# Gated attention mix: the order and form of the first loads, of the first maxima, and of the filler blocks

## The chip, the core and the metric

The kernel runs on one core of a Trainium2 chip. Its time is device time in microseconds (us), the median of several runs. One execution of each kernel is also profiled; the rows shown below come from that execution. TensorE (PE) multiplies matrices into eight PSUM banks of 128x512 fp32, VectorE (DVE) and ScalarE (ACT) read them out, GpSimd (POOL) works between SBUF tiles, and DMA transfers are issued from the queues of SyncE (SP), ACT and POOL.

## The reference

```python
x = A_x                                     # 1 x 2048 x 576, fp32
g = sigmoid((x * gate_w).sum(-1))           # one gate for each row
a = softmax(qa @ ka.T * 18**-0.5) @ va      # 32 heads of 18, each with its own q, k, v
b = softmax(qb @ kb.T * 18**-0.5) @ vb      # 32 heads of 18, with one shared k and v
return g * (a @ A_wo) + (1 - g) * (b @ B_wo)
```

All of it is in fp32. There are 64 heads in all over 2048 keys and 2048 queries; the 32 heads with shared keys come first.

## The kernel before, in words

**Precision and tiling.** A number is split into a high part (the fp32r rounding) and a low part (what the rounding left), and a product is made of three partial products. x comes transposed (576 x 2048). The weights are cut into 14 tiles of 128 output columns ("mt"): tile 0 holds the shared k, the gate, the shared v and the first q rows, tiles 1 to 4 the other q rows of the shared heads, tiles 5 to 13 the q and k rows of the other heads. The contraction over 576 is four chunks of 128 rows and a tail of 64 rows. The tail is loaded twice, into partitions 0 to 63 and 64 to 127 of a fifth chunk, and the upper copy is turned into the low part (`last_x`, `last_w`), so that one matmul does both. `load5` (L244) loads a tile: the four chunks in one transfer ("main"), the tail in two of 64 rows ("rest").

**The first stage** (to about 37 us) projects weight tile 0 for all four column chunks of 512, and tile 1 for the first two. It needs the weight tiles W0 and W1 (`wst`), two x tiles of 256 columns (`xsh`, here x0 and x1) and three of 512 columns (`xs`, here xs2, xs3 and xs4). A tile is split on ACT (high), on DVE (low) and on POOL or DVE (tail). `project` (L265) does one weight tile on one chunk of x, 28 matmuls of 256 columns where `parts` is 2; `leave_first` and `leave` (L295, L290) split the result and write it to memory (`kq`, `kd`, `ke`, `qk`); `first_back` and `rows_back` (L343, L351) read the rows back as the operands of scores (`qs`, `ksb`, `kdb`, `keb`). Both run on SP's queue, which is strictly in order. A DMA that is issued on SP also waits until the transfer eight before it, counted over SP's and ACT's queues together, has landed.

**The lead** (37 to about 75 us) finds row maxima of head 0 and of part of head 1 before the first scores. It is a string of letters (L1142) that `lead_steps` plays. A pair "x", "y" finds the maximum over two key chunks at once: x multiplies with the difference of the two chunks and ACT takes its relu, y multiplies with one chunk and DVE adds the relu and takes the maximum. "A" and "B" are single matmuls of the remaining projections (tile 1's other half, tile 2), on the two halves of the array. `pairs` (L1080) gives the order of the 47 pairs as (first row tile, which two chunks); row tiles 0 to 15 are head 0. After pair (15, 1), `max_rows(0)` turns head 0's maxima into a row that the score matmuls read: DVE, a split on POOL, then two DMAs in a chain, `m_d<-mh` and `qs<-m_d` (L711, L714). "v" makes the shared v.

**The main loop** runs 1024 steps T (16 key tiles of 64 heads). Eight steps are a block: a string of 32 score matmuls "s" (each read out by an exp on ACT), 48 maxima "m" or pairs "x"/"y" for a head 22 steps on (read out by DVE), and the sums over v (the digits). Blocks differ in how many *units* of other work their string holds as A and B: PLAIN none, HALF14 and HALF12 one, TWO14 and TWO12 two, DENSE four. A unit is one 128x292 piece of the other rows' projection (`row_units`), of the values (`value_units`) or of the output projection (`out_proj`). The loop at L1229 picks the string by T. Units for weight tiles 5 to 13 ("the other rows") begin at `RB` = 266, their first loads and splits 8 steps earlier, and `TWICE` gives five of their blocks two units; the output projection begins after `RE` = 730.

Of the kernel before, what the change touches and what calls it, by code (L numbers as in the profile page):

```python
# [8 lines left out]
F32 = mybir.dt.float32  # L9
# [8 lines left out]
S = 2048  # L18
# [138 lines left out]
def gated_mix_kernel(ctx: ExitStack, tc: tile.TileContext, xT, wall, wv, wo, out):  # L157
# [85 lines left out]

    def load5(t, src, rest=None, main=None):  # L244
        dma(t[:, 0:4, :], src[0:512, :].rearrange("(p k) m -> p k m", p=P), main)
        dma(t[0:64, 4, :], src[512:576, :], rest)
        dma(t[64:128, 4, :], src[512:576, :], rest)

    def split_w(st, w, eng_l):
        nc.scalar.activation(w["h"], st, AF.Copy)  # L250
# [88 lines left out]
    def back(t, i, b, x0, x1):  # L339
        n = 64 if i < 3 else 54  # L340
        dma(t[b:b + n, x0:x1], kq_d[54 * i:54 * i + n, x0:x1])

    def first_back():  # L343
        back(ksb, 0, SB, 0, 512)
        back(qs[0], 1, SB, 0, 1024)
        back(qs[0], 1, MB, 0, 1024)
        load_kd(kdb, ROW_KB)
        for b in (MB, SB):
            back(qs[1], 2, b, 0, 1024)

    def rows_back():  # L351
        back(ksb, 0, SB, 1024, 1536)
        dma(keb[MB:MB + 54, :], ke_d.rearrange("p a f -> (p a) f"))
        for b in (MB, SB):
            back(qs[0], 1, b, 1024, S)
        for f in REST_ROWS:
            f()
        for b in (MB, SB):
            back(qs[1], 2, b, 1024, S)
        for b in (SB, MB):  # L360
            for x in (512, 1536):
                back(ksb, 0, b, x, x + 512)
            dma(ksb[b + 54:b + 56, :], ones_r)
        for x in (0, 1024):
            back(ksb, 0, MB, x, x + 512)
        dma(z, z_d.rearrange("(p f) -> p f", p=P))
        for b in (MB, SB):
            back(qs[2], 3, b, 0, S)

    REST_ROWS = []  # L370

    with tc.tile_pool(name="xs", bufs=1, side="right") as xsp:
        XS = []

        def load_x(c, rest=None, main=None):
            half = c < 2
            XS.append(xsp.tile([P, NKT, 256 if half else 512], F32, name="xsh" if half else "xs", bufs=2 if half else 3))
            if main:
                nc.vector.memset(XS[c][0:1, 0:1, 0:1], 0.0)
                nc.vector.memset(XS[c][0:1, 4:5, 0:1], 0.0)  # L380
# [12 lines left out]

        def split_x(c):
            xs = XS[c // 2 + 1][:, :, 256 * (c % 2):256 * (c % 2) + 256] if c > 1 else XS[c]
            cs = slice(c * 256, (c + 1) * 256)
            nc.scalar.activation(X["h"][:, :, cs], xs, AF.Copy)
            low_x(c, xs)
            last_x(c, xs)

        def low_x(c, xs):
            cs = slice(c * 256, (c + 1) * 256)
            nc.vector.tensor_tensor(X["l"][:, :, cs], xs[:, 0:4], X["h"][:, 0:4, cs].bitcast(F32), op=OP.subtract)

        def last_x(c, xs):
            xh = X["h"][64:128, 4, c * 256:(c + 1) * 256]
            (nc.gpsimd if c > 1 else nc.vector).tensor_tensor(xh, xs[64:128, 4], xh.bitcast(F32), op=OP.subtract)

        W = [load_w(0, nc.scalar)]
        load_x(0, nc.scalar)  # L410
        nc.scalar.activation(ones, ones, AF.Copy)
        load_x(1, nc.gpsimd)
        W.append(load_w(1, nc.gpsimd))

        warm = in_turn("m")
        for i in range(6):
            nc.tensor.matmul(warm[:, 0:304], ident, vb.rearrange("p k d -> p (k d)"), start=True, stop=True)
        for c in range(2, 4):
            load_x(c)
        dma(ones_r.rearrange("a (b c) -> (a b) c", c=32), ones)  # L420

        x0, xh = XS[0], X["h"][:, :, 0:256]
        ST = [W.pop(0) for _ in range(2)]
        WP = [main_w(ST[0])]
        nc.scalar.activation(xh[:, 0:2], x0[:, 0:2], AF.Copy)
        nc.vector.tensor_copy(xh[:, 2:4], x0[:, 2:4])
        low_x(0, x0)
        last_w(ST[0], WP[0])
        nc.scalar.activation(xh[:, 4], x0[:, 4], AF.Copy)
        last_x(0, x0)  # L430
        split_x(1)
        WP.append(prep_w(ST[1]))
        load_x(4, nc.gpsimd, nc.gpsimd)
        W.append(load_w(2))

        def chunk(c):
            split_x(2 * c)
            split_x(2 * c + 1)

        F = project(0, 0, WP[0], 2)  # L440
        REST_ROWS.append(leave_first(0, F))
        F = project(1, 0, WP[1], 2)
        chunk(1)
        leave(1, 0, F)
        F = project(0, 1, WP[0], 2)
        REST_ROWS.append(leave_first(1, F))
        first_back()
        F = project(1, 1, WP[1])
        chunk(2)
        leave(1, 1, F)  # L450
        F = project(0, 2, WP[0], 2)
        split_x(6)
        REST_ROWS.append(leave_first(2, F))
        split_x(7)
        F = project(0, 3, WP[0], 2)
        REST_ROWS.append(leave_first(3, F))
        rows_back()
        WP.append(prep_w(W.pop(0)))

# [596 lines left out]
        when(16 * (last_head(t) + 1) + 5, lambda t=t: slow.append(normalise(t)))  # L1056
    when(16 * (NU - 1) + 4, lambda: run(normalise(8, at_end=True)))
    VA = 10 + 8 * (7 * (RA - NT) + 1)
    RB = VA + 8 * 17
    RE = 730  # L1060
    TWICE = [VA + 8 * n for n in range(16)] + [RB + 88 * n for n in range(5)]
    when(2, lambda: begin_units(row_units(NT, RA)))
    when(VA - 8, lambda: (early("vx"), begin_units(value_units())))
    when(RB - 8, lambda: (early("px"), begin_units(row_units(RA, MT))))
    when(RE, open_oacc)
    SEG = ((0, [P] * 4, RE - 8, RE), (4, [P] * 4, 930, 942))
    for t0, rows, Ta, Tb in SEG:
# [5 lines left out]
    def keep_busy():  # L1073

        for n in (512, 256):
# [1 line left out]
                             start=True, stop=True, skip_group_check=True)  # L1077

    pos = {"s": 0, "P": 0, "x": (LEAD + 2) // 2, "y": (LEAD + 2) // 2}
    pairs = {"x": [(M, h) for M0, h in ((0, 0), (16, 0), (0, 1), (8, 0), (8, 1), (16, 1))  # L1080
                   for M in range(M0, M0 + 8)][:-1]}
    pairs["y"] = list(pairs["x"])

# [16 lines left out]
    def lead_max(what, low):  # L1100
        M, h = pairs[what].pop(0)
        u, i = divmod(M, 16)
        b = SB if low else MB
        pm = bank_tile(clk.bank(what, 0 if low else 1))
        k = (kdb, keb)[h][b:b + 54, :] if what == "x" else ksb[b:b + 54, 1024 * h:1024 * h + 512]
        nc.tensor.matmul(pm, qs[u][b:b + 54, i * P:(i + 1) * P], k, start=True, stop=True)  # L1106
        if what == "x":
            MX["x", M, h] = lead.tile([P, 512], F32, name="xb", bufs=2) if (M, h) == (LEAD, 1) else \
                xdp.tile([P, 512], F32, name="xd", bufs=4)
            nc.scalar.activation(MX["x", M, h], pm, AF.Relu)  # L1110
            return
        if u not in MX:
            MX[u] = mxs[u]
        junk = lead.tile([P, 512], BF16, name="junk", bufs=1) if (M, h) == (LEAD, 1) else \
            xdp.tile([P, 512], BF16, name="junk2", bufs=3)
        nc.vector.tensor_tensor_reduce(junk, pm, MX.pop(("x", M, h)), 1.0, -3e38, op0=OP.add, op1=OP.max,  # L1116
                                       accum_out=MX[u][:, i, 2 * h:2 * h + 1])
        if (M, h) == (15, 1):
            max_rows(0)

    def lead_steps(ops):

        for op in ops.replace(" ", ""):
# [12 lines left out]
            else:  # L1136
# [2 lines left out]
    last_m = [(LEAD + 1, 2), (LEAD + 1, 3)]  # L1139
    clk.half = STREAM  # L1140
    begin_units(lead_units())
    lead_steps("xABABxyABxyABABxyABABxyABxyABABxyABABxyABxyABABxyABABxyABxyA"  # L1142
               "BABxyABABxyABxyABABxyABABxyABxyABABxyABABxyABxyABABxyABABxyA"
               "BxyABABxyABABxyABxyABABxyABxyvABABxyABABxyABxyABABxyABABxyAB"
               "xyABABxyABABxyABxyABABxyABABxyABxyABABxyABABxyABABxyABABxyAB"
               "ABxyABxyABByBBBBBssssssmsms")
    clk.half = HALF_MM

    PLAIN = "mssmsm 4 smsmsm 3 smmssx 3 smmsys 3 mssxysm 3 msxmssm 3 mssysms 3 msssmys 4 msmsms 3 smxssm 3"
# [79 lines left out]
    while pos["s"] < 4 * (NSTEP - LEAD):  # L1229
# [3 lines left out]
        if T >= SEG[1][3] + 4:  # L1233
            emit(DENSE, 4)
        elif T in TWICE:
            emit(TWO14, 2)
        elif 10 <= T < RE and T + 8 not in (VA, RB):
            emit(HALF14, 1)
        elif RE + 8 <= T < RE + 8 * 9:
            emit(TWO12, 2)  # L1240
        elif RE + 8 * 9 <= T < RE + 8 * 25:
            emit(HALF12, 1)
        else:
            emit(PLAIN)
# [42 lines left out]
```

## Time and profile before

| what | us |
|---|---|
| median of 3 runs (lowest, highest) | 2651.08 (2648.82, 2652.03) |
| the profiled execution: its time | 2647.61 |
| the profiled execution: its span, first to last instruction | 2645.8 |
| PE busy | 2625.2 (99% of the span) |
| ACT busy | 2448.1 (93%) |
| DVE busy | 2392.7 (90%) |
| POOL busy | 948.4 (36%) |

The granted TensorE clock over the whole span is 0.997 of full speed. A row of the timeline reads: start, duration, engine, line, operation, what is written from what, count, and in brackets the idle time of the engine before it with what ended it. A row of the windows reads: the stretch, its length, busy time and count of each engine, the granted clock, the mean busy share of the 16 DMA engines, and GB/s.

### The profile page before, as it was taken

How to read it: one execution, taken by the hardware profiler on the slowest of the kernel's cores; microseconds unless marked ns; L12 is line 12 of the kernel's file. 1: busy time of each engine (PE TensorE's matmuls, PEld its weight loads, DVE VectorE, ACT ScalarE, POOL GpSimd, SP SyncE). 2: the span in 40 equal slices, each digit the busy share in tenths (PEclk: the TensorE clock that was granted, in tenths of full speed). 3: DMA queues.
4: the chain of work that ended last, by engine and by line, in shares of the span. 5: the costliest groups of instructions: out<-in, count | busy, mean ns of one | idle time of the engine just before them, and what ended most of it. 6: DMA issues, size and time to landing. Idle time of an engine off the chain costs nothing.

```text
span 2645.8 us, 67415 instructions
## 1 busy us (share of the span) xinstructions
PE 2625.2 (99%) x25371; PEld 1412.3 (53%) x25371; DVE 2392.7 (90%) x4571; ACT 2448.1 (93%) x4864; POOL 948.4 (36%) x1195
## 2 busy tenths in 40 slices
PE   8999999999999999999999999999999999999999
PEld 6545555555545455455555555554555554545665
DVE  6899999999989999999999999999989999999883
ACT  6999999999989999999999999999999999999887
POOL 4444331211056454735475447544310020012113
PEclk9999999999999999999999999999999999999999
DMA  7422222221144234333544445434422332223322
GB/s 224 124 84 79 83 78 74 88 63 56 55 126 129 89 103 118 111 104 104 145 141 147 123 120 174 143 103 128 147 86 83 93 98 88 64 84 121 115 57 92
DMA packets 186091, 280.81 MB, mean 106 GB/s; under 512 B 59929, under 2 KB 147305, under 8 KB 174513
## 3 DMA queue, kind: packets, MB, share of 16 engines
q1 hardware_dynamic: 169301, 221.95, 29.2%
q0 software_dynamic: 15424, 53.03, 5.4%
q8 instruction: 200, 3.28, 0.5%
q10 hardware_dynamic: 1040, 1.52, 0.2%
q14 instruction: 126, 1.03, 0.1%
HBM read 200.74 MB, written 66.90 MB: 101 GB/s over the span
## 4 chain that ended last, share of the span: by engine, by line
PE 96%; DMA 1%; POOL 1%; issue 0%; SPq 0%; DVE 0%; ACT 0%; ACTq 0%; POOLq 0%; DVEq 0%
PE acc L749 38%; PE bank L689 28%; PE bank L734 18%; PE bank L957 11%; PE acc L761 1%; PE bank L937 1%; PE bank L1106 0%; DMA m_d<-mh 0%; SPq L163 0%; DMA xst<-xT 0%; DMA qs<-m_d 0%; POOL oacc L930 0%; POOL wrl L242 0%; DVE junk L1116 0%; POOL xr L552 0%
## 5 line engine op out<-in xcount | busy, mean ns | idle before, releaser
L742 ACT ACTIVATE pt<-bank 128x512 f32<-128x512 f32 x4096 | 2153.9, 616 | 143.3 <-PE bank L734 77.1
L698 DVE TENSOR_REDUCE mx<-bank 128x1 f32<-128x512 f32 x3002 | 1890.2, 684 | 138.9 <-PE bank L734 68.9
L734 PE MATMUL bank<-qs,ksb 56*128 56x512 f32 x2688 | 916.2, 425 | 4.3 <-DMA qs<-m_d 4.3
L689 PE MATMUL bank<-ksb,qs 54*128 54x512 f32 x2270 | 821.5, 427 | 0.0
L749 PE MATMUL acc<-pt,vb 128*19 128x128 f32 (+3 forms) x6064 | 552.0, 460 | 0.0
L689 PEld LDWEIGHTS bank<-ksb,qs 54*128 54x128 f32 x2270 | 386.5, 185 | 286.2 <-ACT pt L742 148.1
L749 PE MATMUL acc<-pt,vg 128*19 128x256 f32 (+3 forms) x5936 | 534.6, 456 | 0.0
L734 PEld LDWEIGHTS bank<-qs,ksb 56*128 56x128 f32 x2688 | 443.9, 185 | 167.1 <-DVE mx L698 65.6
L734 PE MATMUL bank<-qs,ksa 56*128 56x512 f32 x1408 | 467.9, 425 | 0.0
L689 PE MATMUL bank<-ksa,qs 54*128 54x512 f32 x1232 | 438.7, 426 | 0.0
L695 DVE CUSTOM_DVE_ANT_0 junk<-bank,xb 128x512 bf16<-128x512 f32 x500 | 342.8, 686 | 30.1 <-PE bank L734 25.5
L692 ACT ACTIVATE xb<-bank 128x512 f32<-128x512 f32 x500 | 294.7, 606 | 12.5 <-PE bank L734 3.8
L689 PEld LDWEIGHTS bank<-ksa,qs 54*128 54x128 f32 x1232 | 207.8, 184 | 151.1 <-ACT pt L742 86.9
L734 PEld LDWEIGHTS bank<-qs,ksa 56*128 56x128 f32 x1408 | 225.8, 184 | 84.7 <-DVE mx L698 31.7
L240 POOL CAST rhl<-rst 128x292 fp32r<-128x292 f32 (+2 forms) x95 | 40.0, 421 | 552.7 <-issue 378.6
L749 PEld LDWEIGHTS acc<-pt,vb 128*19 128x19 f32 x6064 | 122.3, 97 | 215.7 <-issue 186.9
L240 POOL CAST mh<-mt 128x32 fp32r<-128x32 f32 x63 | 13.2, 210 | 614.6 <-DVE mt L707 506.6
L749 PEld LDWEIGHTS acc<-pt,vg 128*19 128x19 f32 x5936 | 119.5, 97 | 208.9 <-issue 183.6
L957 PE MATMUL bank<-xr,wrh 64*128 64x292 f32 (+1 forms) x1386 | 202.9, 300 | 0.0
L957 PEld LDWEIGHTS bank<-xr,wrh 64*128 64x128 f32 x1386 | 169.7, 187 | 3.1
L689 PE MATMUL bank<-kdb,qs 54*128 54x512 f32 x372 | 160.5, 431 | 0.0
L552 POOL TENSOR_TENSOR xr<-xst,xr 128x876 fp32r<-128x876 f32 (+1 forms) x77 | 159.4, 2070 | 0.0
(171 smaller groups left out, 2432.5 us busy)
## 6 DMA issues: line engine op xcount, KB each, us to landing
qs<-qk SPq DMA_DIRECT2D x366, 144.0 KB
xst<-xT SPq DMA_DIRECT2D x66, 438.0 KB
qk<-rhl POOLq DMA_DIRECT2D x66, 292.0 KB, 4.2
ksa<-qk SPq DMA_DIRECT2D x132, 144.0 KB
xst<-xT SPq DMA_DIRECT2D x66, 146.0 KB
xst<-xT SPq DMA_DIRECT2D x132, 73.0 KB
ksb<-qk SPq DMA_DIRECT2D x60, 144.0 KB
onh<-oh POOLq DMA_DIRECT2D x32, 256.0 KB, 3.3
```

The source lines that it names most:

```text
L240: eng_h.tensor_copy(h, src)
L552: nc.gpsimd.tensor_tensor(x[:, 5:8, 0:n], t0, x[:, 0:3, 0:n].bitcast(F32), op=OP.subtract)
L689: nc.tensor.matmul(pm, qs[u % 3][b:b + 54, i * P:(i + 1) * P], k, start=True, stop=True)
L692: nc.scalar.activation(MX["x", u, i], pm, AF.Relu)
L695: nc.vector.tensor_tensor_reduce(junk, pm, MX.pop(("x", u, i)), 1.0, -3e38, op0=OP.add, op1=OP.max, accum_out=MX[u][:, i, c:c + 1])
L698: nc.vector.tensor_reduce(MX[u][:, i, c:c + 1], pm, axis=AX.X, op=OP.max)
L734: nc.tensor.matmul(ps, kst(u)[b:b + 56, i * P:(i + 1) * P], qs[u % 3][b:b + 56, c * 512:(c + 1) * 512], start=True, stop=True)
L742: nc.scalar.activation(pt, ps, AF.Exp, scale=SCALE)
L749: nc.tensor.matmul(acc[32 * j:32 * j + 19, a:b], v_of(u, i), PT[u, i, j][:, a:b], start=(i == 0), stop=(i == 15), skip_group_check=True)
L761: nc.tensor.matmul(acc[32 * j:32 * j + 19, 256 * half + a:256 * half + b], v_of(NU - 1, i), pt[:, x + a:x + b], start=(i == 0), stop=(i == ...
L937: nc.tensor.matmul(fp[:, 0:u.n], x, y, start=(n == 0), stop=(n == len(u.ops) - 1))
L957: nc.tensor.matmul(u.fp[op][:, 0:u.n], x[b:b + 64], y[b:b + 64], start=(n == 0), stop=(n == last))
```

## The change

The line numbers in the program move by up to 7.

- `load5` loads a tail with one transfer of 128 rows, whose source is the 64 rows with a leading dimension of two copies, in place of two transfers of 64 rows. All its callers get this: the first loads, the weight tiles of the other rows (`wrst`), and x for the values.
- W1 and x1 are loaded in the order W0, x0, W1, x1, with all four tails on ACT's queue; W1's and x1's tails were on POOL's. The loads of xs4 and of W2 and the write of `ones_r` are issued later.
- The first projections go tile 0 and tile 1 on x0, then both on x1; two idle matmuls follow. xs4 is split in one piece.
- The reads back go in another order, head 0's first, and `second_back` reads 512 columns earlier.
- In the lead, head 0's 32 pairs come first, `max_rows(0)` splits on DVE, and the A and B stand elsewhere between the pairs.
- `RB` goes from 266 to 274 while the units' first loads stay at T = 258; the block at T = 266 becomes PLAIN; the five extra two-unit blocks become one-unit blocks; `RE` goes from 730 to 778, and 14 blocks of TWO12 and 4 of HALF12 follow in place of 8 and 16.

```diff
     def load5(t, src, rest=None, main=None):
         dma(t[:, 0:4, :], src[0:512, :].rearrange("(p k) m -> p k m", p=P), main)
-        dma(t[0:64, 4, :], src[512:576, :], rest)
-        dma(t[64:128, 4, :], src[512:576, :], rest)
+        m = src.shape[1]
+        dma(t[:, 4, :], src[512:576, :].unsqueeze(0).to_broadcast([2, 64, m]), rest)
...
+    def back2(t, i, x0, x1):
+        for b in (SB, MB):
+            back(t, i, b, x0, x1)
+
     def first_back():
+        back2(qs[0], 1, 0, 1024)
         back(ksb, 0, SB, 0, 512)
-        back(qs[0], 1, SB, 0, 1024)
-        back(qs[0], 1, MB, 0, 1024)
         load_kd(kdb, ROW_KB)
-        for b in (MB, SB):
-            back(qs[1], 2, b, 0, 1024)
+
+    def second_back():
+        back2(qs[0], 1, 1024, 1536)
 
     def rows_back():
+        dma(keb[MB:MB + 54, :], ke_d.rearrange("p a f -> (p a) f"))
+        back2(qs[0], 1, 1536, S)
         back(ksb, 0, SB, 1024, 1536)
...
         W = [load_w(0, nc.scalar)]
         load_x(0, nc.scalar)
+        W.append(load_w(1, nc.scalar))
+        load_x(1, nc.scalar)
         nc.scalar.activation(ones, ones, AF.Copy)
-        load_x(1, nc.gpsimd)
-        W.append(load_w(1, nc.gpsimd))
...
+        WP.append(prep_w(ST[1]))
         split_x(1)
-        WP.append(prep_w(ST[1]))
-        load_x(4, nc.gpsimd, nc.gpsimd)
-        W.append(load_w(2))
...
-        F = project(0, 0, WP[0], 2)
-        REST_ROWS.append(leave_first(0, F))
-        F = project(1, 0, WP[1], 2)
+        F = [in_turn("g") for _ in range(2)]
+        for x in (0, 256):
+            for mt in range(2):
+                products(F[mt], WP[mt], 0, x, 256)
+        idle(2)
+        REST_ROWS.append(leave_first(0, F[0]))
         chunk(1)
-        leave(1, 0, F)
+        load_x(4, nc.gpsimd, nc.gpsimd)
+        leave(1, 0, F[1])
         F = project(0, 1, WP[0], 2)
         REST_ROWS.append(leave_first(1, F))
         first_back()
+        W.append(load_w(2))
+        dma(ones_r.rearrange("a (b c) -> (a b) c", c=32), ones)
         F = project(1, 1, WP[1])
         chunk(2)
         leave(1, 1, F)
         F = project(0, 2, WP[0], 2)
-        split_x(6)
+        chunk(3)
         REST_ROWS.append(leave_first(2, F))
-        split_x(7)
+        second_back()
         F = project(0, 3, WP[0], 2)
...
     VA = 10 + 8 * (7 * (RA - NT) + 1)
-    RB = VA + 8 * 17
-    RE = 730
-    TWICE = [VA + 8 * n for n in range(16)] + [RB + 88 * n for n in range(5)]
+    RB = VA + 8 * 18
+    RE = 778
+    TWICE = [VA + 8 * n for n in range(16)]
...
-    when(RB - 8, lambda: (early("px"), begin_units(row_units(RA, MT))))
+    when(RB - 16, lambda: (early("px"), begin_units(row_units(RA, MT))))
...
-    pairs = {"x": [(M, h) for M0, h in ((0, 0), (16, 0), (0, 1), (8, 0), (8, 1), (16, 1))
+    pairs = {"x": [(M, h) for M0, h in ((0, 0), (8, 0), (0, 1), (8, 1), (16, 0), (16, 1))
                    for M in range(M0, M0 + 8)][:-1]}
...
         if (M, h) == (15, 1):
-            max_rows(0)
+            max_rows(0, nc.vector)
...
-        elif 10 <= T < RE and T + 8 not in (VA, RB):
+        elif 10 <= T < RE and T + 8 not in (VA, RB, RB - 8):
             emit(HALF14, 1)
-        elif RE + 8 <= T < RE + 8 * 9:
+        elif RE + 8 <= T < RE + 8 * 15:
             emit(TWO12, 2)
-        elif RE + 8 * 9 <= T < RE + 8 * 25:
+        elif RE + 8 * 15 <= T < 930:
             emit(HALF12, 1)
```

What moves, at three places. First ACT's queue at the start of the program: wst_118 is W0, xsh_122 (now xsh_121) is x0, xsh_127 is x1, wst_131 (now wst_124) is W1. Before:

```order
L163 DMA wst_118<-wall 64x128 x2
L163 DMA xsh_122<-xT 64x256 x2
L411 ACT_TABLE_LOAD
L411 ACTIVATE ones_96<-ones_96 128x32
L386 ACTIVATE wh_151<-wst_118 128x512
L425 ACTIVATE xh_113<-xsh_122 128x2x256
L391 ACTIVATE wh_151<-wst_118 128x128
L429 ACTIVATE xh_113<-xsh_122 128x256
L397 ACTIVATE xh_113<-xsh_127 128x5x256
L250 ACTIVATE wh_165<-wst_131 128x640
```

With the change:

```order
L163 DMA wst_118<-wall 128x1x128
L163 DMA xsh_121<-xT 128x1x256
L163 DMA wst_124<-wall 128x1x128
L163 DMA xsh_127<-xT 128x1x256
L413 ACT_TABLE_LOAD
L413 ACTIVATE ones_96<-ones_96 128x32
L386 ACTIVATE wh_144<-wst_118 128x512
L428 ACTIVATE xh_113<-xsh_121 128x2x256
L391 ACTIVATE wh_144<-wst_118 128x128
L432 ACTIVATE xh_113<-xsh_121 128x256
L250 ACTIVATE wh_155<-wst_124 128x640
L397 ACTIVATE xh_113<-xsh_127 128x5x256
```

There are still four transfers on ACT's queue, but now one for each tail: x0's is the second, x1's the fourth. ACT splits W1 before x1.

Second, PE's first projections: bank0 is tile 0's result, bank1 tile 1's; wh_151 and wl_152 (now wh_144 and wl_145) are W0, the other pair is W1. Before, from x1's part of tile 0 on:

```order
L277 MATMUL bank0_179<-xh_113,wh_151 128x256 x4
L277 MATMUL bank0_179<-xh_113,wl_152 128x256 x4
L277 MATMUL bank0_179<-xl_114,wh_151 128x256 x4
L277 MATMUL bank0_179<-xh_113,wh_151 128x256
L277 MATMUL bank0_179<-xh_113,wl_152 128x256
L277 MATMUL bank1_218<-xh_113,wh_165 128x256 x4
L277 MATMUL bank1_218<-xh_113,wl_166 128x256 x4
```

With the change, from the same place:

```order
L277 MATMUL bank1_163<-xh_113,wh_155 128x256 x4
L277 MATMUL bank1_163<-xh_113,wl_156 128x256 x4
L277 MATMUL bank1_163<-xl_114,wh_155 128x256 x4
L277 MATMUL bank1_163<-xh_113,wh_155 128x256
L277 MATMUL bank1_163<-xh_113,wl_156 128x256
L277 MATMUL bank0_162<-xh_113,wh_144 128x256 x4
L277 MATMUL bank0_162<-xh_113,wl_145 128x256 x4
```

Tile 1's part on x0 now stands ahead of both parts on x1.

Third, SP's queue where the units of the other rows begin (T = 258 and 266): `wrst` is a weight tile, `xst` a piece of x, `R` and `r_d` belong to a normalisation, `m_d_73` and `qs_92` carry the maxima of head 17, whose scores begin at T = 272. Before:

```order
L163 DMA wrst<-wall 128x512
L163 DMA wrst<-wall 64x128 x2
L163 DMA r_d<-sm 112x128
L163 DMA R<-r_d 16x2048
L163 DMA R<-r_d 18x2048 x6
L163 DMA R<-r_d 4x2048
L163 DMA m_d_73<-mh 128x64
L163 DMA qs_92<-m_d_73 1x64x32 x2
L163 DMA xst<-xT 128x3x292
L163 DMA xst<-xT 128x292
```

With the change:

```order
L163 DMA wrst<-wall 128x512
L163 DMA wrst<-wall 128x1x128
L163 DMA r_d<-sm 112x128
L163 DMA R<-r_d 16x2048
L163 DMA R<-r_d 18x2048 x6
L163 DMA R<-r_d 4x2048
L163 DMA m_d_73<-mh 128x64
L163 DMA qs_92<-m_d_73 1x64x32 x2
L163 DMA qs_91<-qk 18x2048 x6
L163 DMA ot<-oe 18x512 x4
```

Everything up to the maxima of head 17 stands in the order it had, with one transfer fewer; the third piece of x comes after it.

More of the change, by code (lines that the diff above doesn't have):

```diff
@@ L341, in back @@
         dma(t[b:b + n, x0:x1], kq_d[54 * i:54 * i + n, x0:x1])
+    def back2(t, i, x0, x1):
+        for b in (SB, MB):
+            back(t, i, b, x0, x1)
     def first_back():
+        back2(qs[0], 1, 0, 1024)
         back(ksb, 0, SB, 0, 512)
-        back(qs[0], 1, SB, 0, 1024)
-        back(qs[0], 1, MB, 0, 1024)
         load_kd(kdb, ROW_KB)
-        for b in (MB, SB):
-            back(qs[1], 2, b, 0, 1024)
+    def second_back():
+        back2(qs[0], 1, 1024, 1536)
     def rows_back():
+        dma(keb[MB:MB + 54, :], ke_d.rearrange("p a f -> (p a) f"))
+        back2(qs[0], 1, 1536, S)
         back(ksb, 0, SB, 1024, 1536)
-        dma(keb[MB:MB + 54, :], ke_d.rearrange("p a f -> (p a) f"))
-        for b in (MB, SB):
-            back(qs[0], 1, b, 1024, S)
         for f in REST_ROWS:
             f()
-        for b in (MB, SB):
-            back(qs[1], 2, b, 1024, S)
+        back2(qs[1], 2, 0, S)
+        for x in (512, 1536):
+            back(ksb, 0, SB, x, x + 512)
+        back(ksb, 0, MB, 0, S)
         for b in (SB, MB):
-            for x in (512, 1536):
-                back(ksb, 0, b, x, x + 512)
             dma(ksb[b + 54:b + 56, :], ones_r)
-        for x in (0, 1024):
-            back(ksb, 0, MB, x, x + 512)
         dma(z, z_d.rearrange("(p f) -> p f", p=P))
-        for b in (MB, SB):
-            back(qs[2], 3, b, 0, S)
+        back2(qs[2], 3, 0, S)
     REST_ROWS = []
@@ L406, in last_x, with idle @@
             xh = X["h"][64:128, 4, c * 256:(c + 1) * 256]
-            (nc.gpsimd if c > 1 else nc.vector).tensor_tensor(xh, xs[64:128, 4], xh.bitcast(F32), op=OP.subtract)
+            (nc.gpsimd if c > 1 and c % 2 == 0 else nc.vector).tensor_tensor(xh, xs[64:128, 4], xh.bitcast(F32), op=OP.subtract)
         W = [load_w(0, nc.scalar)]
         load_x(0, nc.scalar)
+        W.append(load_w(1, nc.scalar))
+        load_x(1, nc.scalar)
         nc.scalar.activation(ones, ones, AF.Copy)
-        load_x(1, nc.gpsimd)
-        W.append(load_w(1, nc.gpsimd))
         warm = in_turn("m")
-        for i in range(6):
-            nc.tensor.matmul(warm[:, 0:304], ident, vb.rearrange("p k d -> p (k d)"), start=True, stop=True)
+        def idle(n):
+            for i in range(n):
+                nc.tensor.matmul(warm[:, 0:304], ident, vb.rearrange("p k d -> p (k d)"), start=True, stop=True)
+        idle(6)
         for c in range(2, 4):
             load_x(c)
-        dma(ones_r.rearrange("a (b c) -> (a b) c", c=32), ones)
         x0, xh = XS[0], X["h"][:, :, 0:256]
@@ L1141, in gated_mix_kernel @@
     begin_units(lead_units())
[L1142 to L1146, printed above, removed]
+    lead_steps("xABABxyABxyABABxyABxyABABxyABABxyABxyABABxyABABxyABxyABABxyA"
+               "BxyABABxyABABxyvABxyABABxyABABxyABxyABABxyABxyABABxyABABxyAB"
+               "xyABABxyABxyABABxyABABxyABxyABABxyABABxyABxyABABxyABABxyABAB"
+               "xyABABxyABABxyABABxyABABxyABABxyABABxyABABABxyABABxyABABxyAB"
+               "ABxyABBxyBBxyBByBssssssmsms")
     clk.half = HALF_MM
```

## The prediction

> **What bounds the kernel now.** I read the page's chain of waits first, then score matmuls by block, the clock in short windows, and last the timelines of the start.
>
> ```profile
> PE 96%; DMA 1%; POOL 1%; issue 0%; SPq 0%; DVE 0%; ACT 0%; ACTq 0%; POOLq 0%; DVEq 0%
> 354.10:373.51 19.41, 10.65 (x32) 5.21 (x32) 1.00 0.08 24
> 373.51:392.06 18.55, 10.68 (x32) 5.22 (x32) 1.00 0.56 160
> 475.63:496.44 20.81, 11.24 (x32) 5.37 (x32) 1.00 0.20 65
> 1904.55:1925.32 20.77, 11.11 (x32) 5.30 (x32) 1.00 0.45 127
> 2089.32:2108.91 19.59, 10.87 (x33) 5.27 (x33) 1.00 0.22 66
> 744.10:769.82 25.72, 11.91 (x33) 5.65 (x33) 0.93 0.52 141
> 1610.80:1632.35 21.55, 11.32 (x33) 5.37 (x33) 1.00 0.36 99
> 79.63:100.68 21.05, 12.39 (x33) 5.88 (x33) 0.88 0.44 129
> ```
>
> The chain is PE nearly throughout. The other rows are windows of the score line (L734), each one block of 32 score matmuls: HALF14 takes 19.41, PLAIN 18.55, TWO14 20.81, TWO12 20.77, HALF12 19.59 (a late one; its neighbours take 19.4). So a first unit in a block costs about 0.87 and a second about 1.4. Three blocks are off: T = 266 (a TWO14, 25.72), T = 618 (a TWO14, 21.55), and T = 2 (a PLAIN, 21.05). The change touches these and the first stage; between them PE is full and only the mix of blocks counts.
>
> **Part 1: the first loads.** Where the first stage waits now:
>
> ```profile
> 6.52 0.63 ACT L425 ACTIVATE xh<-xsh 128x512 fp32r<-128x512 f32 x1 [0.96 <-DMA xsh<-xT]
> 11.71 0.42 ACT L429 ACTIVATE xh<-xsh 128x256 fp32r<-128x256 f32 x1 [4.36 <-DMA xsh<-xT]
> 12.03 1.25 ACT L397 ACTIVATE xh<-xsh 128x1280 fp32r<-128x1280 f32 x1
> 12.63 0.39 PE L277 MATMUL bank<-xh,wh 128*128 128x256 f32 x1 [3.43 <-DVE xh L407]
> 34.96 0.74 PE L277 MATMUL bank<-xh,wh 128*128 128x256 f32 x4 [1.45 <-ACT xh L397]
> 37.50 0.49 PE L1106 MATMUL bank<-kdb,qs 54*128 54x512 f32 x1 [0.20 <-DMA kdb<-kd]
> ```
>
> x0's main part is there at 6.52, its tail, the last two of ACT's four small transfers, at 11.71, and x1 right behind it; PE loses 3.4 us. The first pair of the lead starts at 37.50. The change wants the tails sooner. What they cost in their new form depends on how many of the 16 DMA engines one transfer uses. The trace has transfers with different outer dimensions almost alone:
>
> ```profile
> 734.00:738.00 4.00, 4.00 (x42) 2.14 (x38) 3.92 (x8) 4.00 (x9) 0.92 (x1) 1.00 0.98 305
> 751.00:757.00 6.00, 6.00 (x62) 3.74 (x60) 5.96 (x11) 5.00 (x10) 1.81 (x4) 1.00 0.57 143
> 61.60:62.50 0.90, 0.90 (x12) 0.77 (x10) 0.90 (x3) 0.79 (x2) 0.71 (x1) 1.00 0.07 18
> q1 hardware_dynamic: 4, 0.02, 7.0%
> ```
>
> With x tiles of 128 rows in flight the engines are 0.98 busy; with `R<-r_d`, whose source is one row broadcast to 18, the share is 0.57, which is 9 of 16, the largest divisor of 18 that 16 engines hold; the third stretch is one `ksb<-ones_r` of 2 rows of 8 KB, the last row its queue: four packets, 7% of 16 engines for 0.90, or 1.0 engine-us, two engines for half a us. So the outer dimension sets the count, a leading broadcast dimension included. The new tail has a source of 2 x 64 rows whose first dimension is a broadcast of 2, and a destination of 128 rows. No row has a transfer whose two sides differ so; I take the smaller side, **two engines**, and keep 16 as a rival. (The Trainium skill, DMA: Bandwidth & Descriptors, in the section "Why a DMA increments its semaphore by 16 and not by 1", says that the number of engines is the largest up to 16 that divides the slowest dimension of both sides, and elsewhere names a leading zero-stride broadcast as what confines a copy. The counts of 9 and 2 above agree with it, and by it the tails run on two engines. It speaks against this change.)
>
> Price: the 2-row transfer moves 8 KB per engine in 0.49 us, 16.6 GB/s; the 128-row window gives 305/(0.98 x 16) = 19.5 GB/s. Two engines carry 31 to 39 GB/s. ACT's four tails are 64 + 128 + 64 + 128 = 384 KB, so 10 to 13 us from the start of transfers near 2, if nothing else uses those engines: x1's tail at 12 at the earliest. But SP's queue uses the same engines: an eighth of its 3584 KB of mains (448 KB) and both 256 KB tails of xs2 and xs3. All 1344 KB would take until 37 to 46. SP holds some of that back, since an issue waits for the landing of the transfer eight before it:
>
> ```profile
> 3.73 8.38 SPq L163 DMA_DIRECT2D xs<-xT  x6
> L163 SPq DMA_DIRECT2D xs<-xT x6: 465/516/1612, 3.7 to 11.6; - x6
> L163 POOL DMA_DIRECT2D xs<-xT x3: 529/534/797, 16.2 to 17.5; - x3
> DMA to landing us min/median/max: 9.0/9.2/9.3
> ```
>
> six issues of about half a us stretch over 8.38, and now xs2 waits for W0's tail and xs3 for x0's. With one packet of SP's between two of ACT's, counted packet by packet, I get W0's tail at 9, x0's at 15, W1's at 22, x1's at 30. I take **30**, with 20 and 39 as ends. PE cannot put it off: both tiles need x1 before anything else can follow. ACT's split of x1 then goes from 12.03 to 30: **+18** (+8 to +27).
>
> From there to the first pair takes 25.5 now. Tile 1's 14 matmuls on x0 are done by then, and x7's split no longer stands behind a readout, which saves most of the 1.45 at 34.96. Against it, xs4's load moves from 16.17, 4.1 after x1's split, to behind the splits of xs2, some 10.3 after it. It took 9.0 to 9.3 to land (last rows above), so ACT, ready for it about 16 after x1, waits till 19.5. Net **+1.5** (0 to +3). Order of reading back: head 0's columns 1024 to 2047 are wanted by pairs 8 and 12, now 16 pairs sooner; their cover is the ten pairs ahead, at 0.7 us each, and if the last read came late it would cost about 1, inside the ends.
>
> **Part 2: the lead's end.**
>
> ```profile
> 71.00 0.35 SPq L163 DMA_DIRECT2D m_d<-mh  x1
> 73.40 1.25 SPq L163 DMA_DIRECT2D qs<-m_d  x2
> 74.28 0.69 DVE L1116 CUSTOM_DVE_ANT_0 junk<-bank,xb 128x512 bf16<-128x512 f32 x1
> 76.41 0.93 PE L734 MATMUL bank<-qs,ksb 56*128 56x512 f32 x3 [1.18 <-DMA qs<-m_d]
> 75.50:77.00 1.50, 0.59 (x4) 0.53 (x5) 0.00 (x0) 0.52 (x2) 0.98 (x1) 1.00 0.81 293
> 78.00:80.00 2.00, 2.00 (x7) 1.44 (x6) 1.38 (x2) 2.00 (x5) 1.66 (x2) 0.50 0.06 25
> 82.00:84.00 2.00, 2.00 (x10) 0.50 (x4) 1.05 (x2) 1.08 (x3) 0.00 (x0) 0.50 0.16 53
> ```
>
> The first score waits 1.18 for the maxima of head 0. About 2 us later the granted clock halves and stays so to about 84; the block at T = 2 takes 21.05, 2.5 over a PLAIN. With head 0's pairs first, `max_rows(0)` stands 15 pairs before the end, 10 us, against the 5.4 from `m_d<-mh` at 71.00 to 76.41, so the DMAs are covered. The split on DVE adds two ops of about 0.2, inside the ends. The sum of A, B, x and y is unchanged. I take **-3.7**: the wait and the slow clock behind it. (The Trainium skill, TensorE: Matmul & The Clock Gate, Part 1, puts the drop behind an idle window of about 3.4 us. The idle stretch here is 1.18 and the clock still falls. By the rule alone only the 1.2 would come back, and the sum below would be +19.3.)
>
> **Part 3: the blocks.** From T = 266 to 922, five TWO14 and twelve HALF12 become ten HALF14, six TWO12 and one PLAIN: 5 x 20.81 + 12 x 19.4 = 336.9 against 10 x 19.41 + 6 x 20.77 + 18.55 = 337.3, or +0.4; the TWO14 at T = 618 was 0.7 over its kind, which goes: -0.3. At T = 266:
>
> ```profile
> 745.20 2.92 SPq L163 DMA_DIRECT2D wrst<-wall  x3
> 752.57 0.34 SPq L163 DMA_DIRECT2D m_d<-mh  x1
> 759.78 1.25 SPq L163 DMA_DIRECT2D qs<-m_d  x2
> 762.60 0.47 PE L734 MATMUL bank<-qs,ksb 56*128 56x512 f32 x1 [3.09 <-DMA qs<-m_d]
> ```
>
> head 17's maxima are issued at 752.57, land 7.2 later behind 1 MB of `R<-r_d`, and PE waits 3.09 at 762.60. SP's order up to there is the same, so the free block does not bring them sooner: it brings PE's need sooner, to 744.1 + 0.75 x 18.55 = 758.0, a wait of 4.6 with 1.5 of slow clock, 24.7 in all for 25.72, of which 20.81 was work. The block's two units are priced above, so its loss over its kind goes from 4.9 to 6.1: +1.2. One issue less on SP gives up to 1 back; W's tail of 64 KB on two engines in front of R costs 1.7 to 2.1. Together **+1** (-4, were the wait gone, to +3).
>
> **The sum.** +18 + 1.5 - 3.7 + 1 = +16.8 on the profiled execution's own time of 2647.6 (span 2645.8 and 1.8 around it): 2664.4. The median of the runs shown stands 3.5 higher, at 2651.08, so I predict **2668** for the median. The tail's break-even is 13 us: landing then, x1 would be 1.2 late, and the sum is zero.
>
> **The rivals.**
> *Faster: the tails run on all 16 engines*, as the destination's 128 rows would have it. Now ACT's fourth transfer is seen at 11.71, 2.7 each from 0.75; as the second, x0's would be there near 7 and PE's 3.4 us wait at 12.63 would go. x1's would still come near 10.9; with xs4 later than now the first pair comes 3.2 sooner. With -3.7 and -1 (no late tail at T = 266): -8, **2643**. For it: the form saves transfers, and the destination is an ordinary one. Against it: the share of 0.57 on a leading broadcast.
> *No change: two engines, but ACT's queue served first.* Then x1's tail lands near 14: +2 + 1.5 - 3.7 + 1 = +0.8, **2652**. For it: 10 to 13 us of bytes are all it needs. Against it: the engines are 0.98 busy when SP's mains run, and the tail's packets must stand in line.
> The free block that removes the wait at 762.60 is worth 4 more on any of these; nothing in SP's order speaks for it.
>
> **How the numbers follow.** Two engines with SP's packets between: 0.68, own range 2657 to 2677 (x1's tail from 20 to 39); 16 engines: 0.22; two engines, short: 0.10. A measurement can tell about 0.2% (5.3 us) from no change. The first case lies above that nearly always (0.66, and 0.02 within), the second below it in 0.19 (0.03 within), the third within in 0.06 and 0.02 on either side. Slower 0.68, same 0.11, faster 0.21. The range of 2643 to 2677 holds some 0.6 of the first case, the third and half of the second, 0.8 in all.
>
> **What would show it.** Right: on ACT, the split of x0's tail begins after 13 and that of x1 (five chunks, 128x1280) near 30, both ended by a DMA; DMA share well under 0.5 between 15 and 30; the first pair near 57; no idle PE before the first score and a T = 2 block near 18.6; T = 266 still waiting for `qs<-m_d`. Wrong: x0's tail split before 9, or x1's before 13; then the outer dimension of the source does not confine a transfer, and the loss of part 1 is a gain.

## The result, and the profile after

The changed kernel takes 2676.12 us (median of four, 2671.24 to 2677.71) against 2649.95 (2646.59 to 2652.03): 1.0097 times as long, with a 95% interval of 1.0079 to 1.0114. It is slower by about 26 us. The forecast was slower, 2668 in a range of 2643 to 2677. Its sum was +16.8 on the profiled execution; that of the changed kernel has a span of 2673.9 (2675.66 with what lies around it), 28.1 more than the 2645.8 before. So the direction and the main cause came out, and 11 us are missing.

The page's chain of waits of the changed kernel, whose share of DMA was 1% before:

```profile
PE 94%; DMA 3%; POOL 1%; DVE 1%; SPq 0%; issue 0%; ACT 0%; ACTq 0%; POOLq 0%
```

The timeline of its first loads and first stage (start, duration, engine, line, and in brackets the idle time before and who ended it), and one window of it (length, busy time of each engine, then clock, DMA share, GB/s). The line of a five-tile split is L397 as before, the first splits of x0 are three lines further down, pairs are L1113, scores L741:

```profile
3.29 6.58 ACTq L163 DMA_DIRECT2D xsh<-xT  x1
13.70 0.42 ACT L432 ACTIVATE xh<-xsh 128x256 fp32r<-128x256 f32 x1 [1.04 <-DMA xsh<-xT]
21.31 0.74 ACT L250 ACTIVATE wh<-wst 128x640 fp32r<-128x640 f32 x1 [7.19 <-DMA wst<-wall]
29.51 1.27 ACT L397 ACTIVATE xh<-xsh 128x1280 fp32r<-128x1280 f32 x1 [7.47 <-DMA xsh<-xT]
25.00:30.00 5.00, 0.46 (x3) 0.17 (x1) 0.00 (x0) 0.49 (x1) 0.00 (x0) 0.84 0.13 47
41.15 1.65 POOL L163 DMA_DIRECT2D xs<-xT  x2 [1.95 <-DVE xs L380]
53.83 2.43 ACT L397 ACTIVATE xh<-xs 128x1280 fp32r<-128x1280 f32 x2 [7.02 <-DMA xs<-xT]
60.66 0.50 PE L1113 MATMUL bank<-kdb,qs 54*128 54x512 f32 x1
```

x0's tail, then W1's, then x1's land one after the other, each ending an idle ACT. From 25 to 30 the DMA share is 0.13, two of 16 engines, at 47 GB/s. x1's tail does not have these two to itself. The queues from 20 to 25 (packets, MB, share of 16 engines):

```profile
q1 hardware_dynamic: 81, 0.16, 9.0%
q10 hardware_dynamic: 82, 0.08, 4.4%
```

q10 is ACT's queue (its 0.39 MB by 29.5 are the four tails), q1 is SP's, where only the tails of xs2 and xs3 have this form. They take turns, packet by packet. ACT itself stands on its fourth issue until 9.87 (first row of the timeline), so its first split, of W0, starts at 11.33 instead of 4.95; what holds the issue the trace does not say, and the late x1 hides it. Then ACT waits again, for xs4, and the first pair starts at 60.66 instead of 37.50.

The lead in the timelines of PE and SP, with one window for the clock:

```profile
69.66 0.26 SPq L163 DMA_DIRECT2D keb<-ke  x1
70.03 1.75 SPq L163 DMA_DIRECT2D qs<-kq  x2
74.28 0.76 PE L1113 MATMUL bank<-kdb,qs 54*128 54x512 f32 x1 [2.75 <-DMA qs<-kq]
76.00:78.00 2.00, 2.00 (x12) 1.22 (x11) 0.93 (x3) 0.96 (x2) 0.00 (x0) 0.50 0.98 298
104.69 0.40 PE L741 MATMUL bank<-qs,ksb 56*128 56x512 f32 x1
```

The first score waits for nothing any more. But in the middle of the lead the thirteenth pair waits 2.75 for the last 512 columns of head 0's queries, and the clock is at half from 74 to 82. The lead, first pair to first score, takes 44.03 where it took 38.91.

Not all of this is the change. One of the kernels below, the probe, differs from the changed kernel only behind its last output. In its execution x1's split and the first pair come at 29.53 and 60.32, nearly as here, but the same pair waits 1.88, the clock stays at 1.00 behind it (it is at half only earlier, from about 66 to 69), and the lead takes 40.75 (its thirteenth pair and its first score):

```profile
74.31 0.47 PE L1113 MATMUL bank<-kdb,qs 54*128 54x512 f32 x1 [1.88 <-DMA qs<-kq]
101.07 1.32 PE L741 MATMUL bank<-qs,ksb 56*128 56x512 f32 x5
```

Blocks, as windows of the score line (the last row is the kernel before, its last block):

```profile
107.85:128.29 20.44, 11.59 (x32) 5.36 (x32) 1.00 0.42 118
771.75:796.82 25.07, 11.77 (x32) 5.61 (x33) 0.86 0.37 104
2584.59:2607.66 23.07, 11.74 (x33) 5.56 (x34) 1.00 0.17 54
2556.36:2579.43 23.07, 11.72 (x32) 5.56 (x32) 1.00 0.17 54
```

T = 2 takes 20.44 with the clock at full speed; T = 266, now a PLAIN, still takes 25.07; T = 618 is an ordinary HALF14 (19.42). The ends of the last blocks, 2607.66 and 2579.43, close the account:

| stretch | before | after | measured | predicted |
|---|---|---|---|---|
| start to x1's split | 12.03 | 29.51 | +17.5 | +18 |
| x1's split to the first pair | 25.47 | 31.15 | +5.7 | +1.5 |
| first pair to first score (the lead) | 38.91 | 44.03 | +5.1 | -1.2 |
| first score to the block at T = 10 | 24.27 | 23.60 | -0.7 | -2.5 |
| T = 10 to the end of the blocks | 2478.75 | 2479.37 | +0.6 | +1 |

### The profile page after: what moved, and what is told of

Its sections match the earlier page's. It is cut to its first block, busy times and chain, and to the rows that moved or that the text cites. A ratio compares the mean times of both kernels' runs of the same rounds, so it can differ in the third digit from the quotient of the medians.

```text
span 2673.9 us, 67473 instructions
## 1 busy us (share of the span) xinstructions
PE 2632.4 (98%) x25439; PEld 1425.0 (53%) x25439; DVE 2393.5 (90%) x4576; ACT 2450.6 (92%) x4864; POOL 941.7 (35%) x1185
## 4 chain that ended last, share of the span: by engine, by line
PE 94%; DMA 3%; POOL 1%; DVE 1%; SPq 0%; issue 0%; ACT 0%; ACTq 0%; POOLq 0%
PE acc L756 37%; PE bank L696 28%; PE bank L741 17%; PE bank L964 10%; DMA xsh<-xT 1%; PE acc L768 1%; PE bank L944 0%; SPq L163 0%; DMA xs<-xT 0%; DMA ksb<-kq 0%; DMA qs<-kq 0%; DMA m_d<-mh 0%; DMA kq<-phl 0%; DVE xl L403 0%; DMA xst<-xT 0%
## 5 line engine op out<-in xcount | busy, mean ns | idle before, releaser
L741 PE MATMUL bank<-qs,ksb 56*128 56x512 f32 x2688 | 914.3, 424 | 4.7 <-DMA qs<-m_d 4.4
L756 PE MATMUL acc<-pt,vb 128*19 128x256 f32 (+3 forms) x6112 | 552.4, 457 | 0.0
L756 PE MATMUL acc<-pt,vg 128*19 128x512 f32 (+3 forms) x5952 | 531.5, 455 | 0.0
L741 PEld LDWEIGHTS bank<-qs,ksb 56*128 56x128 f32 x2688 | 443.2, 184 | 165.0 <-DVE mx L705 65.6
L741 PE MATMUL bank<-qs,ksa 56*128 56x512 f32 x1408 | 467.6, 425 | 0.1
L741 PEld LDWEIGHTS bank<-qs,ksa 56*128 56x128 f32 x1408 | 225.8, 184 | 82.9 <-DVE mx L705 33.0
```

What stands on the lines that cost most here:

```text
L741: nc.tensor.matmul(ps, kst(u)[b:b + 56, i * P:(i + 1) * P], qs[u % 3][b:b + 56, c * 512:(c + 1) * 512], start=True, stop=True)
L756: nc.tensor.matmul(acc[32 * j:32 * j + 19, a:b], v_of(u, i), PT[u, i, j][:, a:b], start=(i == 0), stop=(i == 15), skip_group_check=True)
```

## The experiments

Theory: a tail whose source leads with a broadcast of 2 runs on two DMA engines, and the rest of the loss is the lead's late read and xs4's late load. Rivals: the new order of the loads is at fault, or broadcasts as such are slow.

**Tails in two transfers again, all else changed.**

```diff
-        dma(t[:, 4, :], src[512:576, :].unsqueeze(0).to_broadcast([2, 64, m]), rest)
+        dma(t[0:64, 4, :], src[512:576, :], rest)
+        dma(t[64:128, 4, :], src[512:576, :], rest)
```

> The changed kernel, but every tail of five-tile loads (the first loads and those of W and x in the blocks) again in two transfers of 64 rows; the order of loads, the lead and the blocks stay changed. Theory (the source's leading dimension of 2 put each tail on two engines): the split of x1 on ACT moves from 29.51 to 14 (11 to 18, since eight small transfers now stand in ACT's queue), xs4's tail lands 3 to 4 sooner after its issue, DMA share between 20 and 30 is above 0.5, the first pair comes at 41 to 46 instead of 60.66, and the time falls by 16 to 22, to about 2657. The lead keeps its own loss (a pair waiting 2.75 for the last read-back of head 0's queries), so it stays some 5 above the kernel before's lead. Rival (the loss comes from the new order, four tails on ACT's queue and tiles 0 and 1 in turn, not from the engines): x1's split stays beyond 25 and the time falls by less than 5.

Measured: 2657.6 (2651.3 to 2658.77), 1.0024 times the kernel before (1.0013 to 1.0035). ACT and PE in its timeline, and two windows (all engines; then of the score line at T = 2):

```profile
9.74 1.27 ACT L397 ACTIVATE xh<-xsh 128x1280 fp32r<-128x1280 f32 x1
40.31 0.76 PE L1113 MATMUL bank<-kdb,qs 54*128 54x512 f32 x1 [4.98 <-DMA kdb<-kd]
53.41 0.47 PE L1113 MATMUL bank<-kdb,qs 54*128 54x512 f32 x1 [3.40 <-DMA qs<-kq]
56.00:58.00 2.00, 2.00 (x18) 1.73 (x16) 0.70 (x2) 0.60 (x1) 0.00 (x0) 0.50 0.86 192
84.28 1.32 PE L741 MATMUL bank<-qs,ksb 56*128 56x512 f32 x5
87.44:109.46 22.02, 12.31 (x33) 6.01 (x33) 0.84 0.40 114
```

x1's split moves from 29.51 to 9.74, sooner than expected: the order of the loads on ACT's queue is not at fault, with it x1 is split 2.3 sooner than before. Some 18 of the 26 us are the tails' form (2676.12 to 2657.6). The rest stays: 30.57 from x1's split to the first pair, of which 4.98 is now a wait for `kdb`, and 43.97 in the lead.

**The tail alone, in the kernel before.** The same edit the other way round, and nothing else.

> The kernel before, with nothing changed but the tail of five-tile loads, one transfer with a source of 2 x 64 rows. Theory of two engines: x0's tail split moves from 11.71 to 13 to 16, x1's split from 12.03 to 24 to 30, xs4's tail lands over 11 after its issue instead of 9.2, and the time rises by 12 to 22, to 2662 to 2672. Rival (16 engines, the order of loads is at fault): x0's tail split comes at 7 to 11 and the time stays within 5 of 2650.

Measured: 2665.88 (2662.67 to 2667.81), 1.0059 (1.0041 to 1.0077), about +16.

```profile
17.82 0.42 ACT L429 ACTIVATE xh<-xsh 128x256 fp32r<-128x256 f32 x1 [10.14 <-DMA xsh<-xT]
18.14 1.25 ACT L397 ACTIVATE xh<-xsh 128x1280 fp32r<-128x1280 f32 x1
50.90 0.47 PE L1106 MATMUL bank<-kdb,qs 54*128 54x512 f32 x1 [0.83 <-DMA qs<-kq]
759.90:786.93 27.03, 12.56 (x32) 6.04 (x33) 0.87 0.50 137
```

This single edit makes the kernel slower. How it does so was expected wrongly: x0's tail is the late one (17.82, not 13 to 16), and x1, whose tail comes over POOL's queue here, is there at 18.14, not after 24. The first pair is 13.4 late: 6.1 of it stand ahead of x1's split, and later ACT waits 4.88 for xs3, whose tail has the new form too. T = 266 (last row, its score window) takes 27.03 for 25.72. Yet the two-tail kernel's T = 266 took 25.65 against 25.07 with one transfer, so what the form costs in the blocks stays open, at about a us either way.

**xs4's tail alone in two transfers**, in the changed kernel:

```diff
+        if main:
+            dma(t[0:64, 4, :], src[512:576, :], rest)
+            dma(t[64:128, 4, :], src[512:576, :], rest)
+        else: ...
```

> The changed kernel, with the tail of xs4 alone in two transfers of 64 rows. Theory (xs4's 256 KB tail on two engines is what ACT waits 7.02 for at 53.83): that wait falls by 3 to 4.5, the first pair comes at 56 to 58, and the time falls by about as much, to 2672. Rival (xs4's load is late because it is issued at 41.15, behind the splits of xs2): the wait stays above 6 and the time is unchanged.

Measured: 2677.38 (2671.52 to 2680.69), 1.0101 (1.0082 to 1.012): no gain. ACT and PE:

```profile
49.24 2.44 ACT L401 ACTIVATE xh<-xs 128x1280 fp32r<-128x1280 f32 x2 [2.69 <-DMA xs<-xT]
58.07 0.76 PE L1117 MATMUL bank<-kdb,qs 54*128 54x512 f32 x1 [3.50 <-DMA kdb<-kd]
```

The theory's cause is right, ACT's wait falls from 7.02 to 2.69; its price is not. What stands behind, the wait for `kdb`, is next: 3.50, and only 2.6 come through to the first pair. In the median nothing is seen of them.

**The price of the form by itself (the probe).** Sixteen single transfers behind the last output, into a tile no longer in use, each waiting for the one before; this group for m = 128 and 256, twice:

```diff
+            dma(q1[:, 0:m], xT[0:128, 0:m])
+            dma(q1[:, 0:m], xT[512:576, 0:m].unsqueeze(0).to_broadcast([2, 64, m]))
+            dma(q1[0:64, 0:m], xT[512:576, 0:m])
+            dma(q1[0:64, 0:m], xT[512:513, 0:m].to_broadcast([64, m]))
```

> The changed kernel, with 16 single transfers behind its last output, each waiting for the one before on the same tile: 128 rows, 2 x 64 rows from a leading broadcast, 64 rows, and 64 rows from one broadcast row, of 512 B and of 1 KB each. Theory (the outer dimension of a source sets its engines): the 2 x 64 transfer of 128 KB takes 2.5 to 4 longer to land than the 128 rows of the same bytes, that of 64 KB 1.2 to 2 longer, and the one row broadcast to 64 is as quick as 64 rows within 0.3. Rival (a broadcast as such is slow): the row broadcast to 64 is slow too. Rival (16 engines for all): all four lie within 0.5.

SP's timeline; a transfer's time is the distance to the next row. The first four rows are of 1 KB a row (128 rows, 2 x 64, 64, and 64 from one), the next three of 512 B (128 rows, 2 x 64, 64):

```profile
2679.65 0.34 SPq L163 DMA_DIRECT2D vb<-xT  x1
2682.12 0.58 SPq L163 DMA_DIRECT2D vb<-xT  x1
2687.21 0.49 SPq L163 DMA_DIRECT2D vb<-xT  x1
2689.64 0.47 SPq L163 DMA_DIRECT2D vb<-xT  x1
2692.15 0.33 SPq L163 DMA_DIRECT2D vb<-xT  x1
2694.18 0.55 SPq L163 DMA_DIRECT2D vb<-xT  x1
2697.75 0.49 SPq L163 DMA_DIRECT2D vb<-xT  x1
```

128 KB: 2.47 as 128 rows, 5.09 as 2 x 64. 64 KB: 2.03 and 3.57. Of the other round, the 2 x 64 rows took 4.93 and 3.41 and the 128 rows of 1 KB 2.35; its 128 rows of 512 B ran while the outputs were still being written. The one row broadcast to 64 takes 2.51, the 64 rows 2.43: a broadcast as such costs next to nothing, a leading dimension of 2 does. From 64 to 128 KB the form takes 1.52 longer, 43 GB/s, where I had 31 to 39. (The Trainium skill, DMA: Bandwidth & Descriptors, in the section "Why a DMA increments its semaphore by 16 and not by 1", takes the largest number up to 16 that divides the slowest dimension of both sides, here 2. The DMA share of 0.13 above, two of 16, and the 5.09 against 2.47 agree with it.)

**xs4 early**, on the two-tail kernel:

```diff
         split_x(1)
+        load_x(4, nc.gpsimd, nc.gpsimd)
...
         chunk(1)
-        load_x(4, nc.gpsimd, nc.gpsimd)
```

> The kernel of two 64-row tails, with the load of xs4 issued where the kernel before has it, right behind the split of x1 and ahead of the splits of xs2. Theory (the late xs4 load is under way while tile 0's first results are written and read back, and kdb is late by that): the wait of 4.98 for kdb ahead of the first pair falls below 2, ACT's wait of 2.18 for xs4 goes, the first pair comes at 35 to 37.5 instead of 40.31, and the time falls by 3 to 5, to 2653. Rival (the read-back is late by SP's own order, which now holds W's third tile and both halves of the queries): the wait for kdb stays above 4 and the time is the same within 2.

Measured: 2652.54 (2650.38 to 2657.34), 1.0011 (1.0002 to 1.0021). The first two rows are POOL's issue of xs4 in the two-tail kernel and here; then ACT and PE here:

```profile
22.16 1.88 POOL L163 DMA_DIRECT2D xs<-xT  x3 [1.96 <-DVE xs L380]
14.03 2.04 POOL L163 DMA_DIRECT2D xs<-xT  x3 [12.72 <-DVE xs L380]
9.83 1.27 ACT L397 ACTIVATE xh<-xsh 128x1280 fp32r<-128x1280 f32 x1
34.85 0.47 PE L1113 MATMUL bank<-kdb,qs 54*128 54x512 f32 x1 [0.53 <-DMA kdb<-kd]
```

The wait for `kdb` falls from 4.98 to 0.53 and the first pair comes 5.46 sooner, at 34.85; from x1's split it is 25.02, the 25.47 of before. So the late load of xs4 holds up the reading back of tile 0's results. SP's order is the same in both kernels. The DMA share between 27 and 31 falls from 0.95 to 0.43 without the 1280 KB of xs4 there, and SP reads back at 28.75 instead of 32.91. The lead keeps its late read, a wait of 3.92.

**keb's read behind the queries'**, on the two-tail kernel:

```diff
-        dma(keb[MB:MB + 54, :], ke_d.rearrange("p a f -> (p a) f"))
         back2(qs[0], 1, 1536, S)
+        dma(keb[MB:MB + 54, :], ke_d.rearrange("p a f -> (p a) f"))
```

> The kernel of two 64-row tails, with the read of keb behind the read of head 0's last 512 query columns instead of ahead of it. Theory (SP stands for keb's write to land and so issues the queries' read 2 later than it could): the wait of 3.40 of the pair at 53.41 falls to 1.4 (0 to 2), the half clock behind it shortens, the lead from first pair to first score goes from 43.97 to 40 to 42, and the time falls by 2 to 4, to 2654.5. Rival (the read is late by its own transfer, 4.3 from issue to use in a busy stretch): the wait stays above 3 and the time is the same within 2.

Measured: 2653.36 (2649.31 to 2657.53), 1.0013 (1.0004 to 1.0022). PE, with one window:

```profile
39.81 0.76 PE L1113 MATMUL bank<-kdb,qs 54*128 54x512 f32 x1 [3.58 <-DMA kdb<-kd]
51.55 0.47 PE L1113 MATMUL bank<-kdb,qs 54*128 54x512 f32 x1 [2.04 <-DMA qs<-kq]
52.00:54.00 2.00, 2.00 (x24) 1.61 (x20) 1.81 (x5) 1.74 (x3) 0.59 (x1) 1.00 0.68 188
79.62 0.92 PE L741 MATMUL bank<-qs,ksb 56*128 56x512 f32 x3 [1.14 <-DMA qs<-m_d]
```

The wait falls from 3.40 to 2.04, and the clock stays at 1.00 behind it. The lead takes 39.81 instead of 43.97: 4.2 less for 1.4 less of waiting. How much of this is keb's place stays open, since the changed kernel's lead differed by 3.3 between two executions with nothing moved. Ahead of the queries' read, keb's went with waits of 3.40 and, with xs4 early, 3.92; behind it with 2.04 and, in the next kernel, 1.24. At the end of this quicker lead the wait for the maxima is back, 1.14. The medians of these two kernels and of the two-tail kernel lie within each other's spread, so what the two edits bring is read from the timelines alone.

**All three, and the maxima ahead of R.** The second normalisation starts six steps later, so that SP issues the next head's maxima ahead of its eight R reads:

```diff
-        when(16 * (last_head(t) + 1) + 5, lambda t=t: slow.append(normalise(t)))
+        when(16 * (last_head(t) + 1) + (11 if t == 1 else 5), lambda t=t: slow.append(normalise(t)))
```

> Two 64-row tails, xs4 early, keb's read behind the queries', and the second normalisation started 6 steps later, so that its 1 MB of R reads stands behind the maxima of the next head in SP's queue. Theory (the T = 266 wait is the maxima standing behind R): no PE wait for the maxima in T = 266 and a block of 18.6 to 19.6 instead of 25.65; with the two front terms the time is 2644 (2638 to 2650), below both kernels. Rival (the maxima are late by the wait for the free W buffer ahead of them, not by R): T = 266 stays above 23 and the time stays above 2648.

Measured: 2644.36 (2642.66 to 2649.58), 0.9984 (0.9975 to 0.9993): faster than the changed kernel and than the kernel before, which took 2650.3 beside it. PE in its lead, SP at T = 266 (in the changed kernel R was issued at 774.21 and the maxima behind it at 780.27), and that block's score window:

```profile
36.58 0.47 PE L1113 MATMUL bank<-kdb,qs 54*128 54x512 f32 x1 [0.64 <-DMA kdb<-kd]
49.59 0.47 PE L1113 MATMUL bank<-kdb,qs 54*128 54x512 f32 x1 [1.24 <-DMA qs<-kq]
76.95 0.93 PE L741 MATMUL bank<-qs,ksb 56*128 56x512 f32 x3 [0.40 <-DMA qs<-m_d]
750.31 0.37 SPq L163 DMA_DIRECT2D m_d<-mh  x1
754.33 3.15 SPq L163 DMA_DIRECT2D R<-r_d  x8
747.21:765.74 18.53, 10.67 (x32) 5.22 (x32) 1.00 0.41 106
```

T = 266 takes 18.53 instead of 25.07, and no PE wait for the maxima is left in it. The free block alone could not do that; the order in SP's queue does.

**That one line in the kernel before.**

> The kernel before, with nothing changed but the second normalisation started 6 steps later, so that its R reads stand behind the next head's maxima. It tells how much of the 6 us by which the last kernel beats the kernel before is this one line. Theory (the front and the lead of the change, mended, give back what they take: its first score comes 0.5 later than before's): T = 266, a TWO14, takes 20.8 instead of 25.72, and the time is 2645.5 (2643 to 2648), the same as the 2644.36 of the mended change within 2. Rival (the mended front and lead hold a gain of their own that the one profile hides): this kernel stays at 2647 or above, and the mended change is faster by 3 or more.

Measured: 2645.69 (2643.78 to 2649.3), 0.9987 (0.9978 to 0.9996). Its T = 266, a TWO14:

```profile
746.37:767.25 20.88, 11.24 (x32) 5.38 (x32) 1.00 0.65 137
```

T = 266 is 4.84 shorter, and the median 4.85 shorter than the 2650.54 of the kernel before beside it. One line gives what the whole mended change gives: 0.9987 against 0.9984, with intervals that overlap. The first loads, the lead and the free blocks, mended, are worth nothing that can be measured. Ahead of T = 266 this kernel is the kernel before, yet its first score comes at 78.57 behind a wait of 2.93, not at 76.41 behind 1.18. Differences of some 2 us between single executions, like the 2.6 that xs4's tail brought, show little there.

## Why the prediction was right, and where not

**The tails (+18, measured +17.5): right, by the mechanism named.** x0's tail split after 13 (13.70), x1's near 30 (29.51), the DMA share from 15 to 30 at 0.34 and from 20 at 0.13, and the two queues taking turns packet by packet (81 and 82). The estimate of W1's tail at 22 (21.31) fits too. That the packet count hits this well is partly luck. W0's tail was put at 9, but ACT's queue had moved its 64 KB by 5.2; the next tail took 8.5 more where 6 were counted; and in the kernel before with the new tail alone the same reasoning missed both tiles. Both rivals of the prediction fell, 16 engines and ACT's queue served first.

**From x1 to the first pair (+1.5, measured +5.7): mis-sized.** I priced xs4's later load as ACT's wait alone and took its landing, 9.0 to 9.3, from the old form; its own 256 KB tail now runs on two engines too, which the part on tails should have carried over. With that tail mended most of the loss stays, since the reading back waits for the same engines: with xs4's tail alone in two transfers 28.68, with two tails everywhere 30.57, with xs4 early 25.02.

**The lead's end (-3.7): failed, in both of its halves.** The wait of 1.18 did go, in the changed kernel. But "if the last read came late it would cost about 1" was the step that failed: the read came 2.75 late and the clock halved behind the wait, so that the lead took +5.1 against the -1.2 of the sum. In the probe's execution it came 1.88 late, the clock stayed up behind it, and the lead took +1.8. That `keb` stood ahead of the read in SP's queue is a likely part of the cause, but the runs do not set it apart from the differences between executions. And most of T = 2's excess over a PLAIN is not the clock: at 1.00 it takes 20.44, 0.6 less than before's 21.05, not 2.5; what the other 1.9 are no run shows. Nor is the half clock there bound to the wait ahead of the first score, as the term had it: the clock fell without any such wait too (last section). (The Trainium skill, TensorE: Matmul & The Clock Gate, Part 1, lets the clock fall after an idle window of about 3.4 us. It gave the nearer price for T = 2, and in the lead 2.04 left the clock at 1.00 and 3.40 halved it; but 2.75 halved it too, and the falls in the last section do not fit it.)

**The blocks (+1, measured +0.6): right.** The wait at T = 266 stayed as worked out, 4.39 for 4.6, and the block took 25.07 for 24.7:

```profile
789.80 0.76 PE L741 MATMUL bank<-qs,ksb 56*128 56x512 f32 x1 [4.39 <-DMA qs<-m_d]
```

That the maxima were late for standing behind R was only argued there; the last two experiments show it.

In all the sum was 11.4 short on the profiled execution: 4.2 in the reading back, 6.3 in the lead (3.3 of them not in the probe's execution), 1.8 at T = 2, less 0.9 in the other two.

## What to carry to other kernels

Before two transfers are made into one, look at the outermost dimension of both sides: a leading 2 puts everything on two engines, and the transfer saved costs far more than it brings. When a load or a read moves in a queue, price it against everything that shares the engines or the queue behind it, not only its own reader. And where PE waits for a small transfer, look at what stands ahead of it in its queue before moving work on PE. Before a few us of a single execution are explained, see what a second execution of the same code does.

## What was not expected of the hardware

A short wait can cost several times its length through the clock: of two executions of the changed kernel's lead, the one that waited 0.9 us less, with some 3 us of half clock in place of 8 or more, was 3.3 shorter. No length of wait can be given from which on it falls. In the middle of the lead 2.04 and 1.88 left it at 1.00, and 2.75 brought 0.50 for about 8 us; but in the kernel with everything mended a wait of 1.12, which began 1.4 us behind one of 0.64, was followed by the half clock as well (PE's timeline and a window):

```profile
39.09 0.50 PE L1113 MATMUL bank<-kdb,qs 54*128 54x512 f32 x1 [1.12 <-ACT pst L307]
42.00:44.00 2.00, 2.00 (x13) 1.76 (x11) 1.61 (x5) 1.19 (x2) 0.00 (x0) 0.50 0.67 212
```

And in the two-tail kernel the clock fell near T = 2 (the mean of 0.84 in its window above) with no wait of PE ahead of it in the timeline. With xs4 early it did so again, behind a first score at 79.94 that waited for nothing:

```profile
84.00:86.00 2.00, 2.00 (x12) 0.51 (x11) 0.72 (x3) 2.00 (x7) 1.24 (x3) 0.50 0.17 53
```

In the changed kernel's T = 2, and in the probe's, it did not fall. What brings that about stays open.
